# B step of a two-block recurrent transformer: Q b in one pass, half a's scores directly behind it, half b's maximum by a TensorE product, fewer mask and memory products, tail unit split

## The chip, the cores and the metric

The kernel runs on 1 core of one Trainium2 chip. The metric is the device time of one execution in microseconds (us). TensorE (PE) does the matrix products and writes PSUM; VectorE (DVE), ScalarE (ACT) and GpSimd (POOL) do the rest; SyncE (SP) issues most DMA.

## What is computed

Four layers A, B, A, B on x of [1, 2048, 640], each with a layer norm ahead and a residual sum behind. A is an attention in four segments with a linear memory; the change does not touch it. B is a segment recurrence, cut here to what matters:

```python
mem = mem0                                   # [1, 8, 640]
for s in range(n_seg):                       # 64 segments of 32 tokens
    h = concatenate([mem, xs], axis=1)       # 40 rows: 8 of memory, 32 of the segment
    q, k, v = h @ Wq, h @ Wk, h @ Wv         # 32 heads of 128
    scores = where(mask, q @ k.T * scale, -1e9)  # mask: row < 8 or row >= column
    p = softmax(scores)
    o = (p @ v) @ Wo
    mem = o[:, :M, :].copy()                 # the next step needs this
    outs.append(o[:, M:, :])
```

So the 64 steps of a B layer follow each other strictly: the memory rows of a step come out of its output product.

## The kernel before

A B step s (function layer_B, loop over 64 steps) holds the segment's columns as b_HX, [128, 5 chunks of 640, 32 columns]: 24 tokens known ahead and 8 memory columns written last. The other 8 tokens of each segment (the "tails") do not depend on the recurrence; they are projected ahead, four steps at once, by one "unit" a step: tail_unit (K or Q of a half, 20 products of 512 columns, PSUM tile b_tail, copied by ScalarE to b_tu in tail_evac and transposed by VectorE into b_tK or b_tQ in tail_turn) and vtail_unit (V, tile b_vtail, cut into pieces by vtail_some and stored by DMA). The output rows of the tails are deferred too (od_chunk, tile b_OPSd).

The 32 heads stand in two halves, a (0 to 15) and b (16 to 31). In PSUM, 32 rows of four column groups j carry four heads at a time: a product with tile_position=(0, 32 * j) uses the 128 x 32 part j of TensorE's array, and four of them run side by side (written 128*32 in the profile).

The order of a step on TensorE, ScalarE, VectorE and GpSimd is the order of the program: layer_B runs under _OrdNC, which chains the instructions of each engine. TensorE's order in a step before the change:

1. K a, Q a, K b (by_head, 20 products of 512 columns each: b_Ka, b_Qa, b_Kb), Q b in two passes of 256 columns (b_Qb in the ps pool, b_Qc in the tail buffer). kq copies each by ScalarE to b_kq, turn transposes it by VectorE into b_KT or b_QT.
2. mask_mm of half a (four 128*32 products of the identity with the mask, tile b_SP), one chunk of V a (thin_mm, b_Va), the 32 score products of half a (b_KT with b_QT and b_QZ), two chunks of V a, mask_mm and scores of half b with one chunk of V a between, the last chunk.
3. V b (b_Vb), od_chunk (b_OPSd), the whole tail unit (b_tail), and in some steps ln_spread (five 128*128 transposes, b_lntps).
4. pv of half a (b_OTP from b_PTa), pv of half b (from b_PTb): products of 32*128 and 8*128. Two chunks of vtail.
5. The output product (b_OPS, 64 products), the second part of od_chunk, then the memory rows: ScalarE copies three pieces of b_OPS to b_msb, TensorE sums and transposes each with the selection matrix selm (b_MT), VectorE copies it into the next step's b_HX; vtail chunks stand between.

The softmax of a half on the way from b_SP to b_PT: soft_max (VectorE, negated row maximum, b_negmax), soft_sub (VectorE, adds it into PSUM), soft_exp (ScalarE, b_E), soft_sum and soft_rec (VectorE, b_ssum, b_rs), soft_p (GpSimd, b_Pn), p_turn (two transposes on VectorE, b_PTa or b_PTb). VectorE's order before is: soft_max, soft_sub of a, then of b, then soft_sum and soft_rec of a and of b, then p_turn of a and b.

Layer-norm units: ln_begin (VectorE statistics) stands in steps with s % 4 == 1 (up to 57) and in three steps with s % 16 == 10, 18 of 64; ln_spread follows one step later. In steps 0 to 59 there is a tail unit to be kept, in 60 to 62 one runs without use, in 63 none.

Of the kernel before, what the change touches and what calls it, by code (L numbers as in the profile page):

```python
# [18 lines left out]
F32 = mybir.dt.float32  # L19
BF16 = mybir.dt.bfloat16  # L20
ACT = mybir.ActivationFunctionType
ALU = mybir.AluOpType
# [784 lines left out]
def layer_B(nc, tc, C, W, x_src, xb_src, x_dst, mem0, B_Wv, B_Wo, nsteps=64, out_bf16=False, tag=""):  # L807
# [6 lines left out]
    with ExitStack() as ctx:  # L814
# [26 lines left out]
        def ps_tile(shape, dtype, name):  # L841
            return pp.tile(shape, dtype, name=name, tag="ps")
# [72 lines left out]
        def thin_mm(cols_ap, Wt, b, name, c0=0, c1=NCH, ps=None):  # L915
            if ps is None:
                ps = ps_tile([128, 512], F32, name)
            for c in range(c0, c1):
                for j in range(4):
                    n = 4 * b + j  # L920
                    nc.tensor.matmul(ps[32 * j:32 * j + 32, :], lhsT=cols_ap[:, c, :], rhs=Wt[:, c, 512 * n:512 * n + 512],
                                     start=(c == 0), stop=(c == NCH - 1), tile_position=(0, 32 * j), skip_group_check=True)
            return ps

        def by_head(cols_ap, Wt, h0, nh, ps):
            for c in range(NCH):
                wt = Wt[:, c, 128 * h0:128 * (h0 + nh)].rearrange("p (h e) -> p h e", e=128)
                for j in range(4):
                    nc.tensor.matmul(ps[32 * j:32 * j + 32, :].rearrange("p (h x) -> p h x", x=32), lhsT=cols_ap[:, c, :], rhs=wt[:, :, 32 * j:32 * j + 32],
                                     start=(c == 0), stop=(c == NCH - 1), tile_position=(0, 32 * j), skip_group_check=True)  # L930
            return ps
# [16 lines left out]
        def tail_cols(g, c=None):  # L948
            v = TX[g // 4][:, :, 4 * (g % 4):4 * (g % 4) + 4, :].rearrange("p c s t -> p c (s t)")
            return v if c is None else v[:, c]  # L950

        def tail_unit(g, k, ps):
            proj, b = divmod(k, 2)
            return by_head(tail_cols(g), W.wq if proj else W.wk, 16 * b, 16, ps)

        def tail_evac(k, ps):
            sb = kqp.tile([128, 512], BF16, name="b_tu", tag="kq")
            evac("act", sb[:], ps[:], SCB if k // 2 else None)
            return sb
# [130 lines left out]
        for s in range(nsteps):  # L1090
# [11 lines left out]
            def kq(ps, scale=None, n=512, name="b_kq"):  # L1102
                sb = kqp.tile([128, n], BF16, name=name, tag="kq")
                evac("act", sb[:], ps[:], scale)
                return sb

            def turn(sb, D_, h0, nh):
                nc.vector.transpose(out=D_[s][:, h0:h0 + nh, 0:32], in_=sb[:].rearrange("p (h x) -> p h x", x=32))

            def mask_mm(b):  # L1110
                SP = ps_tile([128, 5, 40], F32, f"b_SP{b}")
                for j in range(4):
                    nc.tensor.matmul(SP[32 * j:32 * j + 32].rearrange("p g k -> p (g k)"), lhsT=C.identb[:, 32 * j:32 * j + 32], rhs=mask5[:].rearrange("p g k -> p (g k)"),
                                     start=True, stop=False, tile_position=(0, 32 * j), skip_group_check=True)
                return SP

            def scores(b, SP):
# [6 lines left out]
                            nc.tensor.matmul(SP[32 * j:32 * j + 32, 0 if tail else 1 + i, :], lhsT=lhsT, rhs=KT[s][:, h, :],  # L1124
                                             start=False, stop=True, tile_position=(0, 32 * j), skip_group_check=True)

            negmax = sm.tile([128, 2, 5], F32, name="b_negmax", tag="negmax")
            ssum = sm.tile([128, 2, 5], F32, name="b_ssum", tag="ssum")
            rs = sm.tile([128, 2, 5], F32, name="b_rs", tag="rs")
            E_ = wk.tile([128, 2, 5, 40], BF16, name="b_E", tag="E0")  # L1130

            def soft_max(b, SP):
                nc.vector.tensor_reduce(out=negmax[:, b, :], in_=SP[:], axis=AX.X, op=ALU.max, negate=True)

            def soft_sub(b, SP):
                nc.vector.tensor_tensor(out=SP[:], in0=SP[:], in1=negmax[:, b, :].unsqueeze(2).to_broadcast([128, 5, 40]), op=ALU.add)

            def soft_exp(b, SP):
                nc.scalar.activation(out=E_[:, b], in_=SP[:], func=ACT.Exp)

            def soft_sum(b):
                nc.vector.tensor_reduce(out=ssum[:, b, :], in_=E_[:, b], axis=AX.X, op=ALU.add)

            def soft_rec(b):
                nc.vector.reciprocal(out=rs[:, b, :], in_=ssum[:, b, :])

            def soft_p(eng, b):
                eng.tensor_tensor(out=Pn[:, b, :, 0:40], in0=E_[:, b], in1=rs[:, b, :].unsqueeze(2).to_broadcast([128, 5, 40]), op=ALU.mult)

            def p_turn(b, PT):  # L1150
                nc.vector.transpose(out=PT[:, :, :, 8:40], in_=Pn[:, b, 1:5, :].rearrange("p g (a k) -> p a g k", a=2))
                nc.vector.transpose(out=PT[:, :, :, 0:8], in_=Pn[:, b, 0, :].rearrange("p (a i t) -> p a i t", a=2, i=4))
# [19 lines left out]
            VH[s] = wkl.tile([128, 2, 512], BF16, name="b_Vth", tag="Vth")  # L1172
            for b in range(2):
                for nm, Wt, D_, scale in (("K", W.wk, KT, None), ("Q", W.wq, QT, SCB)):
                    if b and nm == "Q":
                        for e, q in enumerate((ps_tile([128, 256], F32, "b_Qb"), po.tile([128, 256], F32, name="b_Qc", tag="tail"))):
                            by_head(cols, Wt, 16 + 8 * e, 8, q)
                            turn(kq(q, scale, 256), D_, 16 + 8 * e, 8)
                    else:
                        ps = by_head(cols, Wt, 16 * b, 16, ps_tile([128, 512], F32, f"b_{nm}{'ab'[b]}"))  # L1180
                        turn(kq(ps, scale), D_, 16 * b, 16)
            SPa = mask_mm(0)
            Va = thin_mm(cols, W.wv, 0, "b_Va", 0, 1)
            scores(0, SPa)
            thin_mm(cols, W.wv, 0, "b_Va", 1, 3, Va)
            SPb = mask_mm(1)
            thin_mm(cols, W.wv, 0, "b_Va", 3, 4, Va)
            scores(1, SPb)
            thin_mm(cols, W.wv, 0, "b_Va", 4, NCH, Va)
            PTa = wkl.tile([128, 2, 4, 40], BF16, name="b_PTa", tag="PTa")  # L1190
            PTb = wkl.tile([128, 2, 4, 40], BF16, name="b_PTb", tag="PTb")
            soft_max(0, SPa)
            soft_sub(0, SPa)
            soft_exp(0, SPa)
            soft_max(1, SPb)
            soft_sub(1, SPb)
            soft_sum(0)
            soft_rec(0)
            soft_p(nc.gpsimd, 0)
            soft_exp(1, SPb)  # L1200
            evac("act", VH[s][:, 0, :], Va[:])
            soft_sum(1)
            soft_rec(1)
            soft_p(nc.gpsimd, 1)
            p_turn(0, PTa)
            p_turn(1, PTb)
            Vb = thin_mm(cols, W.wv, 1, "b_Vb")
            evac("act", VH[s][:, 1, :], Vb[:])
            if not last:
                od_chunk(0)  # L1210

            if work:
                tps = tail_unit(work[0], work[1], po.tile([128, 512], F32, name="b_tail", tag="tail"))
            if unit:
                tsb = tail_evac(unit[1], tps)
            if ln_ready:
                ln_spread(ln_ready.pop(0), po.tile([128, NCH, 4, 32], BF16, name="b_lntps", tag="ops"))
            if last:
# [9 lines left out]
            OTv = OTsb[:].rearrange("p (a x) -> p a x", a=2)  # L1228
            pv(0, PTa, ots)
            evac("dve", OTv[:, 0, 0:160], otf[0][:].rearrange("p i c -> p (i c)"))  # L1230
            ot01 = ps_tile([128, 4, 40], F32, "b_OTP1")
            ots[0][1] = ot01[:]
            pv(1, PTb, ots)
            evac("act", OTv[:, :, 160:320], otf[1][:].rearrange("p a i c -> p a (i c)"))
            evac("dve", OTv[:, 1, 0:160], ot01[:].rearrange("p i c -> p (i c)"))
            evac("act", OTv[:, :, 480:640], otf[3][:].rearrange("p a i c -> p a (i c)"))
            evac("dve", OTv[:, :, 320:480], otf[2][:].rearrange("p a i c -> p a (i c)"))
            if not last and (s + 1) % 4:
                vtails_in(s + 1)
# [17 lines left out]
            if not last:  # L1257
                dst = cols_of(s + 1)
                msb = wk.tile([128, 320], BF16, name="b_msb", tag="msb")
                parts = ((0, 1), (1, 3), (3, NCH))  # L1260
                for ca, cb in parts:
                    nc.scalar.copy(msb[:, 64 * ca:64 * cb], ops[:, 64 * ca:64 * cb])
                for pi, (ca, cb) in enumerate(parts):
                    mt = ps_tile([128, cb - ca, 8], F32, f"b_MT{pi}")
                    for c in range(ca, cb):
                        for q in range(4):
                            o = 64 * c + 32 * (q % 2)
                            nc.tensor.matmul(mt[32 * q:32 * q + 32, c - ca, :], lhsT=msb[:, o:o + 32], rhs=selm[:, q // 2, :],
                                             start=True, stop=True, tile_position=(0, 32 * q), skip_group_check=True)
                    nc.vector.tensor_copy(dst[:, ca:cb, 24:32], mt[:])  # L1270
                    vtail_some((1, 1, NCH)[pi])
            vtail_some(NCH)
# [114 lines left out]
```

## Time and profile before

| | |
|---|---|
| three timed runs, us | 2427.61, 2425.11, 2420.36 (median 2425.11) |
| the profiled execution, us | 2418.85 |
| its span, first to last instruction, us | 2417.1 |
| granted TensorE clock, mean | 0.997 |
| PE busy | 2289.2 us (95%), 62330 products |
| DVE busy | 1882.4 us (78%) |
| ACT busy | 1416.2 us (59%) |
| POOL busy | 749.8 us (31%) |
| the chain that ended last | PE 67%, DVE 14%, ACT 9%, DMA 4% of the span |

All of it comes from one profiled execution. A busy PE is not PE at its peak: products are pipelined, the profile's length of one product holds the time in which it drains (some 0.17 us), and the next of the same shape starts before that ends. In rows of the timeline the first two columns are the start in the span and the length of the merged row; x20 is the count of instructions in it; a bracket tells how long the engine had stood idle and what released it.

### The profile page before, as it was taken

The numbers are of one execution on the slowest core, as the hardware profiler recorded it, in microseconds if no ns is written. First come the engines' busy times: TensorE is split into PE (matmuls) and PEld (weight loads), VectorE is DVE, ScalarE is ACT, GpSimd is POOL, SyncE is SP. The second block draws the span as 40 slices with busy tenths as digits, with TensorE's granted clock in tenths as the row PEclk, the third lists the DMA queues.
The fourth block names the chain that finished last, engine by engine and source line by source line (L and its number), as shares of the span: only waits on it lengthen the run. The fifth ranks groups of instructions, "written<-read, shape, count | busy, mean of one in ns | idle before, by whom it ended". The sixth has DMA issues, their size and how long they took to land.

```text
span 2417.1 us, 139330 instructions
## 1 busy us (share of the span) xinstructions
PE 2289.2 (95%) x62330; PEld 1504.1 (62%) x62330; DVE 1882.4 (78%) x4695; ACT 1416.2 (59%) x3198; POOL 749.8 (31%) x1589
## 2 busy tenths in 40 slices
PE   8999999999999999999989999999999999999998
PEld 5566656666666666666655665566666666666665
DVE  8999877777777777777679998777777777777776
ACT  6999964444444444444369999644444444445443
POOL 5677641111111111111146776411111111111111
PEclk9999999999999999999999999999999999999999
DMA  4121271111111111111220211711111111111110
GB/s 168 47 85 60 73 260 27 28 32 32 29 30 30 31 29 32 29 31 28 65 88 17 64 45 38 274 24 26 29 28 27 27 27 28 27 29 29 27 24 20
DMA packets 168883, 123.38 MB, mean 51 GB/s; under 512 B 104652, under 2 KB 153180, under 8 KB 166492
## 3 DMA queue, kind: packets, MB, share of 16 engines
q1 hardware_dynamic: 167288, 112.69, 16.4%
q8 instruction: 487, 7.98, 1.4%
q10 hardware_dynamic: 996, 1.79, 0.2%
q14 instruction: 112, 0.92, 0.1%
HBM read 79.60 MB, written 34.80 MB: 47 GB/s over the span
## 4 chain that ended last, share of the span: by engine, by line
PE 67%; DVE 14%; ACT 9%; DMA 4%; issue 3%; POOL 1%; SPq 1%; ACTq 0%; DVEq 0%; POOLq 0%
PE b_OPS L113 11%; PE b_Ka L113 6%; PE b_Kb L113 5%; PE b_Qa L113 5%; DVE a_nm L142 5%; PE b_tail L113 5%; PE b_Va L113 4%; PE b_Vb L113 4%; ACT a_PT L142 4%; PE b_vtail L113 4%; PE a_S L113 3%; PE b_SP L113 2%; PE b_OPSd L113 2%; PE b_OTP L113 2%; PE b_Qb L113 2%
## 5 line engine op out<-in xcount | busy, mean ns | idle before, releaser
L113 PEld LDWEIGHTS <-b_HX 128*32 128x32 bf16 x17920 | 467.0, 96 | 269.0 <-DVE b_HX L113 3.6
L113 POOL TENSOR_TENSOR b_Pn<-b_E,b_rs 128x200 bf16<-128x200 bf16 x256 | 133.4, 522 | 1092.7 <-DVE b_rs L113 1074.6
L142 DVE TENSOR_REDUCE a_nm<-a_S 128x2 f32<-128x512 f32 (+3 forms) x512 | 395.4, 817 | 52.8 <-PE a_S L113 37.5
L142 ACT ACTIVATE a_PT<-a_T 128x1024 bf16<-128x1024 f32 (+1 forms) x384 | 345.5, 905 | 22.8 <-PE a_T L113 15.0
L113 PE MATMUL b_OPS<-b_wo,b_OTsb 128*32 128x320 bf16 x8192 | 306.5, 300 | 4.6 <-DVE b_OTsb L113 3.6
L113 PEld LDWEIGHTS <-b_OTsb 128*32 128x32 bf16 x8192 | 208.1, 96 | 73.8 <-DVE b_OTsb L113 24.8
L113 DVE STREAM_TRANSPOSE b_KT<-b_kq 128x512 bf16<-128x512 bf16 x256 | 181.3, 708 | 80.3 <-ACT b_kq L113 79.7
L142 POOL TENSOR_SCALAR_AFFINE_SELECT a_PT<-a_PT 128x256 bf16<-128x256 bf16 x380 | 189.3, 503 | 152.5 <-ACT a_PT L142 151.0
L113 ACT ACTIVATE b_E<-b_SP 128x200 bf16<-128x200 f32 x256 | 86.3, 337 | 235.5 <-DVE b_SP L113 225.4
L113 PE MATMUL b_Va<-b_wv,b_HX 128*32 128x512 bf16 x2560 | 222.4, 381 | 0.0
L113 DVE CAST b_HX<-b_MT 128x16 bf16<-128x16 f32 (+1 forms) x380 | 64.7, 172 | 198.3 <-PE b_MT L113 190.0
L113 DVE STREAM_TRANSPOSE b_QT<-b_kq 128x256 bf16<-128x256 bf16 (+1 forms) x384 | 184.2, 505 | 39.3 <-ACT b_kq L113 35.9
L113 ACT CAST b_msb<-b_OPS 128x64 bf16<-128x64 f32 x378 | 69.3, 256 | 213.2 <-PE b_OPS L113 213.2
L113 PEld LDWEIGHTS <-b_TX 128*32 128x32 bf16 x5360 | 144.1, 96 | 58.4 <-issue 5.3
L113 DVE CAST b_OTsb<-b_OTP 128x160 bf16<-128x160 f32 (+1 forms) x384 | 133.8, 376 | 44.7 <-PE b_OTP L113 40.8
L113 PE MATMUL b_Ka<-b_wk,b_HX 128*32 128x512 bf16 x2560 | 163.5, 381 | 1.0 <-DVE b_HX L113 0.9
L113 PE MATMUL b_Vb<-b_wv,b_HX 128*32 128x512 bf16 x2560 | 162.2, 379 | 0.0
L113 PE MATMUL b_Qa<-b_wq,b_HX 128*32 128x512 bf16 x2560 | 161.1, 379 | 0.0
L113 PE MATMUL b_Kb<-b_wk,b_HX 128*32 128x512 bf16 x2560 | 161.1, 379 | 0.0
L113 PE MATMUL b_vtail<-b_wv,b_TX 128*32 128x256 bf16 x2680 | 149.7, 273 | 1.3 <-issue 0.7
L113 ACT CAST b_kq<-b_Ka 128x512 bf16<-128x512 f32 x128 | 74.9, 585 | 123.0 <-PE b_Ka L113 123.0
L113 ACT CAST b_OTsb<-b_OTP 128x320 bf16<-128x320 f32 x256 | 96.5, 429 | 81.4 <-PE b_OTP L113 81.0
(185 smaller groups left out, 5048.3 us busy)
## 6 DMA issues: line engine op xcount, KB each, us to landing
b_wv<-in_B_Wv_dram SPq DMA_DIRECT2D x10, 1024.0 KB
b_wo<-in_B_Wo_dram SPq DMA_DIRECT2D x16, 640.0 KB
b_VT<-b_VTd SPq DMA_DIRECT2D x504, 16.0 KB
b_XO<-xres SPq DMA_DIRECT2D x256, 30.0 KB
b_VTd<-b_vt SPq DMA_DIRECT2D x480, 16.0 KB
b_xt<-xres_bf SPq DMA_DIRECT2D x40, 160.0 KB
b_wk<-in_B_Wk_dram SPq DMA_DIRECT2D x20, 256.0 KB
b_wq<-in_B_Wq_dram SPq DMA_DIRECT2D x20, 256.0 KB
```

The source lines that it names most:

```text
L113: r = f(*a, **k)
L142: r = f(*a, **k)
```

## The change

Q b is one pass of 512 columns in one PSUM tile, like the other projections. Its transpose on VectorE comes behind half a's mask, scores and maximum; V a follows in one piece, then mask and scores of half b. Half b's maximum is kept in bf16, and soft_sub of half b is a TensorE product of the identity with the broadcast maximum, accumulated onto b_SP between V b's third and fourth chunk. mask_mm is one 128 x 128 product in place of four of 128 x 32. The tail unit's chunks 0 to 2 stand ahead of pv of half a and chunks 3 and 4 between pv of half a and of half b; its ScalarE copy moves behind the value products' evacuations on ScalarE. p_turn of half a is issued ahead of soft_p of half b. b_MT is made of two 128 x 64 products a chunk in place of four of 128 x 32.

```diff
@@ -922,8 +922,8 @@
                                      start=(c == 0), stop=(c == NCH - 1), tile_position=(0, 32 * j), skip_group_check=True)
             return ps
 
-        def by_head(cols_ap, Wt, h0, nh, ps):
-            for c in range(NCH):
+        def by_head(cols_ap, Wt, h0, nh, ps, c0=0, c1=NCH):
+            for c in range(c0, c1):
                 wt = Wt[:, c, 128 * h0:128 * (h0 + nh)].rearrange("p (h e) -> p h e", e=128)
                 for j in range(4):
                     nc.tensor.matmul(ps[32 * j:32 * j + 32, :].rearrange("p (h x) -> p h x", x=32), lhsT=cols_ap[:, c, :], rhs=wt[:, :, 32 * j:32 * j + 32],
@@ -949,9 +949,9 @@
             v = TX[g // 4][:, :, 4 * (g % 4):4 * (g % 4) + 4, :].rearrange("p c s t -> p c (s t)")
             return v if c is None else v[:, c]
 
-        def tail_unit(g, k, ps):
+        def tail_unit(g, k, ps, c0=0, c1=NCH):
             proj, b = divmod(k, 2)
-            return by_head(tail_cols(g), W.wq if proj else W.wk, 16 * b, 16, ps)
+            return by_head(tail_cols(g), W.wq if proj else W.wk, 16 * b, 16, ps, c0, c1)
 
         def tail_evac(k, ps):
             sb = kqp.tile([128, 512], BF16, name="b_tu", tag="kq")
@@ -1109,9 +1109,8 @@
 
             def mask_mm(b):
                 SP = ps_tile([128, 5, 40], F32, f"b_SP{b}")
-                for j in range(4):
-                    nc.tensor.matmul(SP[32 * j:32 * j + 32].rearrange("p g k -> p (g k)"), lhsT=C.identb[:, 32 * j:32 * j + 32], rhs=mask5[:].rearrange("p g k -> p (g k)"),
-                                     start=True, stop=False, tile_position=(0, 32 * j), skip_group_check=True)
+                nc.tensor.matmul(SP[:].rearrange("p g k -> p (g k)"), lhsT=C.identb[:], rhs=mask5[:].rearrange("p g k -> p (g k)"),
+                                 start=True, stop=False, skip_group_check=True)
                 return SP
 
             def scores(b, SP):
@@ -1124,16 +1123,20 @@
                             nc.tensor.matmul(SP[32 * j:32 * j + 32, 0 if tail else 1 + i, :], lhsT=lhsT, rhs=KT[s][:, h, :],
                                              start=False, stop=True, tile_position=(0, 32 * j), skip_group_check=True)
 
-            negmax = sm.tile([128, 2, 5], F32, name="b_negmax", tag="negmax")
+            negmax = [sm.tile([128, 5], dt_, name=f"b_negmax{b}", tag=f"negmax{b}") for b, dt_ in enumerate((F32, BF16))]
             ssum = sm.tile([128, 2, 5], F32, name="b_ssum", tag="ssum")
             rs = sm.tile([128, 2, 5], F32, name="b_rs", tag="rs")
             E_ = wk.tile([128, 2, 5, 40], BF16, name="b_E", tag="E0")
 
             def soft_max(b, SP):
-                nc.vector.tensor_reduce(out=negmax[:, b, :], in_=SP[:], axis=AX.X, op=ALU.max, negate=True)
+                nc.vector.tensor_reduce(out=negmax[b][:], in_=SP[:], axis=AX.X, op=ALU.max, negate=True)
 
             def soft_sub(b, SP):
-                nc.vector.tensor_tensor(out=SP[:], in0=SP[:], in1=negmax[:, b, :].unsqueeze(2).to_broadcast([128, 5, 40]), op=ALU.add)
+                shift = negmax[b][:].unsqueeze(2).to_broadcast([128, 5, 40])
+                if b:
+                    nc.tensor.matmul(SP[:], lhsT=C.identb[:], rhs=shift, start=False, stop=True, skip_group_check=True)
+                else:
+                    nc.vector.tensor_tensor(out=SP[:], in0=SP[:], in1=shift, op=ALU.add)
 
             def soft_exp(b, SP):
                 nc.scalar.activation(out=E_[:, b], in_=SP[:], func=ACT.Exp)
@@ -1172,47 +1175,41 @@
             VH[s] = wkl.tile([128, 2, 512], BF16, name="b_Vth", tag="Vth")
             for b in range(2):
                 for nm, Wt, D_, scale in (("K", W.wk, KT, None), ("Q", W.wq, QT, SCB)):
-                    if b and nm == "Q":
-                        for e, q in enumerate((ps_tile([128, 256], F32, "b_Qb"), po.tile([128, 256], F32, name="b_Qc", tag="tail"))):
-                            by_head(cols, Wt, 16 + 8 * e, 8, q)
-                            turn(kq(q, scale, 256), D_, 16 + 8 * e, 8)
-                    else:
-                        ps = by_head(cols, Wt, 16 * b, 16, ps_tile([128, 512], F32, f"b_{nm}{'ab'[b]}"))
-                        turn(kq(ps, scale), D_, 16 * b, 16)
+                    ps = by_head(cols, Wt, 16 * b, 16, ps_tile([128, 512], F32, f"b_{nm}{'ab'[b]}"))
+                    sb = kq(ps, scale)
+                    if not (b and nm == "Q"):
+                        turn(sb, D_, 16 * b, 16)
             SPa = mask_mm(0)
-            Va = thin_mm(cols, W.wv, 0, "b_Va", 0, 1)
             scores(0, SPa)
-            thin_mm(cols, W.wv, 0, "b_Va", 1, 3, Va)
+            soft_max(0, SPa)
+            turn(sb, QT, 16, 16)
+            Va = thin_mm(cols, W.wv, 0, "b_Va")
             SPb = mask_mm(1)
-            thin_mm(cols, W.wv, 0, "b_Va", 3, 4, Va)
             scores(1, SPb)
-            thin_mm(cols, W.wv, 0, "b_Va", 4, NCH, Va)
+            soft_sub(0, SPa)
+            soft_max(1, SPb)
+            soft_exp(0, SPa)
+            Vb = thin_mm(cols, W.wv, 1, "b_Vb", 0, 3)
             PTa = wkl.tile([128, 2, 4, 40], BF16, name="b_PTa", tag="PTa")
             PTb = wkl.tile([128, 2, 4, 40], BF16, name="b_PTb", tag="PTb")
-            soft_max(0, SPa)
-            soft_sub(0, SPa)
-            soft_exp(0, SPa)
-            soft_max(1, SPb)
             soft_sub(1, SPb)
+            soft_exp(1, SPb)
+            thin_mm(cols, W.wv, 1, "b_Vb", 3, NCH, Vb)
             soft_sum(0)
             soft_rec(0)
             soft_p(nc.gpsimd, 0)
-            soft_exp(1, SPb)
             evac("act", VH[s][:, 0, :], Va[:])
             soft_sum(1)
             soft_rec(1)
+            p_turn(0, PTa)
             soft_p(nc.gpsimd, 1)
-            p_turn(0, PTa)
             p_turn(1, PTb)
-            Vb = thin_mm(cols, W.wv, 1, "b_Vb")
             evac("act", VH[s][:, 1, :], Vb[:])
             if not last:
                 od_chunk(0)
 
             if work:
-                tps = tail_unit(work[0], work[1], po.tile([128, 512], F32, name="b_tail", tag="tail"))
-            if unit:
-                tsb = tail_evac(unit[1], tps)
+                tps = tail_unit(work[0], work[1], po.tile([128, 512], F32, name="b_tail", tag="tail"), 0, 3)
             if ln_ready:
                 ln_spread(ln_ready.pop(0), po.tile([128, NCH, 4, 32], BF16, name="b_lntps", tag="ops"))
             if last:
@@ -1228,12 +1225,16 @@
             OTv = OTsb[:].rearrange("p (a x) -> p a x", a=2)
             pv(0, PTa, ots)
             evac("dve", OTv[:, 0, 0:160], otf[0][:].rearrange("p i c -> p (i c)"))
+            if work:
+                tail_unit(work[0], work[1], tps, 3, NCH)
             ot01 = ps_tile([128, 4, 40], F32, "b_OTP1")
             ots[0][1] = ot01[:]
             pv(1, PTb, ots)
             evac("act", OTv[:, :, 160:320], otf[1][:].rearrange("p a i c -> p a (i c)"))
             evac("dve", OTv[:, 1, 0:160], ot01[:].rearrange("p i c -> p (i c)"))
             evac("act", OTv[:, :, 480:640], otf[3][:].rearrange("p a i c -> p a (i c)"))
+            if unit:
+                tsb = tail_evac(unit[1], tps)
             evac("dve", OTv[:, :, 320:480], otf[2][:].rearrange("p a i c -> p a (i c)"))
             if not last and (s + 1) % 4:
                 vtails_in(s + 1)
@@ -1263,10 +1264,9 @@
                 for pi, (ca, cb) in enumerate(parts):
                     mt = ps_tile([128, cb - ca, 8], F32, f"b_MT{pi}")
                     for c in range(ca, cb):
-                        for q in range(4):
-                            o = 64 * c + 32 * (q % 2)
-                            nc.tensor.matmul(mt[32 * q:32 * q + 32, c - ca, :], lhsT=msb[:, o:o + 32], rhs=selm[:, q // 2, :],
-                                             start=True, stop=True, tile_position=(0, 32 * q), skip_group_check=True)
+                        for q in range(2):
+                            nc.tensor.matmul(mt[64 * q:64 * q + 64, c - ca, :], lhsT=msb[:, 64 * c:64 * c + 64], rhs=selm[:, q, :],
+                                             start=True, stop=True, tile_position=(0, 64 * q), skip_group_check=True)
                     nc.vector.tensor_copy(dst[:, ca:cb, 24:32], mt[:])
                     vtail_some((1, 1, NCH)[pi])
             vtail_some(NCH)
```

## The prediction

> **What bounds the kernel now.** I read the page first, then the chain of waits in the middle of the second B layer, then the timeline of each engine over one step. The span:
>
> ```profile
> span 2417.1 us, 139330 instructions
> ```
>
> The profiled execution took 2418.85 us, 1.75 us more than this span. The three timed runs have a median of 2425.11 us, 0.3% above it; 0.3%, some 7 us, is also the least difference that a measurement here can tell from none. My sums start from 2418.85.
>
> Two layers of 64 B steps fill most of the span. One step on TensorE's timeline, from its K product to the next one's, with the end of the step in full (columns: start in us, length in us):
>
> ```profile
> 1825.93 1.26 PE L113 MATMUL b_Ka<-b_wk,b_HX 128*32 128x512 bf16 x20
> ...
> 1838.16 0.45 PE L113 MATMUL b_OPSd<-b_wo,b_OTdef 128*32 128x320 bf16 x8
> 1838.44 0.28 PE L113 MATMUL b_vtail<-b_wv,b_TX 128*32 128x256 bf16 x4
> 1838.65 0.19 PE L113 MATMUL b_MT<-b_sel,b_msb 128*32 128x8 bf16 x4
> 1838.69 0.28 PE L113 MATMUL b_vtail<-b_wv,b_TX 128*32 128x256 bf16 x4
> 1838.82 0.21 PE L113 MATMUL b_MT<-b_sel,b_msb 128*32 128x8 bf16 x8
> 1838.89 0.28 PE L113 MATMUL b_vtail<-b_wv,b_TX 128*32 128x256 bf16 x4
> 1839.00 0.21 PE L113 MATMUL b_MT<-b_sel,b_msb 128*32 128x8 bf16 x8
> 1839.12 1.26 PE L113 MATMUL b_Ka<-b_wk,b_HX 128*32 128x512 bf16 x18
> ```
>
> A step takes 1839.12 - 1825.93 = 13.19 us. The chain of waits through the same step:
>
> ```profile
> 1829.35 0.55 PE b_Qb L113 x19
> 1829.90 0.54 PE b_Qc L113 x19
> 1830.44 0.09 PE b_SP L113 x4
> ...
> 1833.53 1.09 PE b_tail L113 x20
> ...
> 1835.42 0.38 PE b_OTP L113 x32
> ```
>
> TensorE has no gap until the tail unit ends at 1834.62. The second value product (the b_OTP at 1835.42) then waits for the softmax, which is VectorE's chain:
>
> ```profile
> 1830.08 0.71 DVE L113 STREAM_TRANSPOSE b_KT<-b_kq 128x512 bf16<-128x512 bf16 x1 [0.35 <-ACT b_kq L113]
> 1830.71 0.73 DVE L113 STREAM_TRANSPOSE b_QT<-b_kq 128x256 bf16<-128x256 bf16 x2
> 1831.47 0.37 DVE L113 TENSOR_REDUCE b_negmax<-b_SP 128x5 f32<-128x200 f32 x1
> 1831.88 0.37 DVE L113 TENSOR_TENSOR b_SP<-b_SP,b_negmax 128x200 f32<-128x200 f32 x1
> ...
> 1833.39 0.36 DVE L113 TENSOR_REDUCE b_ssum<-b_E 128x5 f32<-128x200 bf16 x1
> 1833.78 0.19 DVE L113 RECIPROCAL b_rs<-b_ssum 128x5 f32<-128x5 f32 x1
> 1834.12 0.57 DVE L113 STREAM_TRANSPOSE b_PTa<-b_Pn 128x256 bf16<-128x256 bf16 x2
> 1834.70 0.57 DVE L113 STREAM_TRANSPOSE b_PTb<-b_Pn 128x256 bf16<-128x256 bf16 x2
> ```
>
> VectorE works without a pause from 1830.08 to 1835.27, and b_OTP starts 0.15 us later. So two paths are nearly balanced: TensorE's full order, and VectorE's chain, which makes TensorE wait some half a microsecond.
>
> **The price that decides: a change of tile shape on TensorE.** Three places of the timeline, two of TensorE around a step with a layer-norm unit and one at the start of the first B layer. The figure before the sizes (128*32, 128*128, 32*128) is the part of the array that a product occupies:
>
> ```profile
> 1807.61 0.62 PE L113 MATMUL b_tail<-b_wq,b_TX 128*32 128x512 bf16 x8
> 1808.16 0.45 PE L113 MATMUL b_lntps<-c_identb,b_xt 128*128 128x128 bf16 x5
> 1808.55 0.20 PE L113 MATMUL b_OTP<-b_PTa,b_Vth 32*128 32x40 bf16 x4
> ...
> 1809.22 0.20 PE L113 MATMUL b_OTP<-b_PTb,b_VT 8*128 8x40 bf16 x4
> 1809.39 0.40 PE L113 MATMUL b_vtail<-b_wv,b_TX 128*32 128x256 bf16 x8
> ```
>
> ```profile
> 341.78 0.84 PE L113 MATMUL a_YP<-a_wo,a_oTx 128*128 128x320 bf16 x5 [0.37 <-DVE a_late L142]
> 342.55 2.34 PE L113 MATMUL b_tail<-b_wk,b_TX 128*32 128x512 bf16 x39
> ```
>
> Between products of one shape, the next starts 0.17 us before the last has ended: OPSd ends at 1838.16 + 0.45 = 1838.61 and vtail starts at 1838.44. Where the shape changes the overlap shrinks: b_tail (128*32) ends at 1808.23 and b_lntps (128*128) starts at 1808.16, 0.07 before; from b_lntps to b_OTP 0.06; from b_OTP back to 128*32 0.03 (1809.42 against 1809.39); from the A layer's 128*128 to b_tail's 128*32 0.07 (342.62 against 342.55). A change of shape thus costs TensorE 0.10, 0.11, 0.14 and 0.10 us. I take 0.11.
>
> The Trainium skill has this as a rule ("TensorEngine Tiling (Array Packing)", Tiling Modes, Key Properties): changing the tiling mode, and not just the tile, drains TensorE. The trace agrees for the three shapes above; the page also lists 128×64 as a mode of its own, which no row here shows.
>
> **The change part by part**, for a step without a layer-norm unit, in the times of the step at 1825.93.
>
> Q b in one pass: 1.08 like the other 512-wide products (Vb to OPSd or Ka to the next), in place of 0.55 + 0.54. -0.01 us; Q b ends at 1830.43.
>
> Masks: four 128*32 products side by side (0.09) become one 128*128 product. It streams the same 200 columns, so again 0.09, but the array changes to the full shape and back: +0.22 each, twice, +0.44. None of it is hidden: TensorE has work queued on both sides.
>
> Half a's scores directly behind Q b: 1830.43 + 0.31 (mask) + 0.23 for 32 score products, as now, gives 1830.97. VectorE's maximum of half a then comes before the transpose of Q b. That transpose waits for ScalarE's copy, 0.60 us long from about 1830.53:
>
> ```profile
> 1828.39 0.60 ACT L113 ACTIVATE b_kq<-b_Qa 128x512 bf16<-128x512 f32 x1 [0.50 <-PE b_Qa L113]
> ...
> 1833.02 0.34 ACT L113 ACTIVATE b_E<-b_SP 128x200 bf16<-128x200 f32 x1 [0.32 <-DVE b_SP L113]
> ```
>
> So: maximum at 1831.04, transpose of Q b from 1831.4 to 1832.1. Queued behind it on VectorE are half a's subtraction and half b's maximum. TensorE meanwhile does all of Va (1.08, to 1832.05) and the second mask (to 1832.36), so half b's scores do not wait; they end at 1832.59.
>
> Half b's maximum by a TensorE product: VectorE loses one subtraction (0.38), TensorE gains a full-shape product of 200 columns: 0.09 + 0.22 = +0.31. It is placed behind 12 of Vb's 20 products (0.65). The maximum of half b is ready at about 1833.03, before TensorE arrives at 1833.24, so nothing waits for it, and what is queued behind it (the rest of Vb) is not held up. The product ends at 1833.44. The shift is a broadcast operand of step 0, of which no row shows the speed: at worst I allow a second 0.09, at best nothing more.
>
> From there the chain to the second value product: exponential of half b about 0.10 later, 1833.54; its sum 0.37 after that start (1833.02 to 1833.39 now), 1833.91; reciprocal 0.39 on, 1834.30; transposes of half a behind it from 1834.49 to 1835.06 (GpSimd's product of half a is finished by then); those of half b 0.92 after the reciprocal's start, as now, 1835.22 to 1835.79.
>
> TensorE: the tail unit's first 12 products end at 1834.62 - 0.01 + 0.44 + 0.31 - 0.43 = 1834.93. The first value product waits for its transposes: 1835.06 + 0.05 = 1835.11, and ends at 1835.49. Then the shape changes to 128*32 for the tail unit's last 8 products (0.11 + 0.43, to 1836.03) and back (0.11, less the overlap of 0.17): the second value product starts at 1835.97, now bound by TensorE and not by VectorE (1835.79 + 0.15 = 1835.94). Against 1835.42 that is +0.55 us. What stood in TensorE's wait before is more than used up.
>
> The memory products (b_MT) become half as many, each 128*64, between vtail products of 128*32. The first change of shape is free: b_vtail's four products take 0.11 (1838.89 to 1839.00), so TensorE is idle by 1838.55 and b_MT waits until 1838.65 for ScalarE. Five changes remain before the next Ka: 0.55. Against it stand 0.08 for halved products (half of 0.04 + 0.07 + 0.05) and 0.07 of slack before Ka, which waits for the first b_HX copy. +0.40 us. Bounds: -0.02 if 64 columns need no change, +0.55 at 0.14 a change. I take 0.11, the row nearest to it, since every change of columns in the trace costs about that.
>
> The tail unit's ScalarE copy and VectorE transpose (0.70) move behind the evacuations of the value products, some 0.73 us later in VectorE's queue. Queued behind are a layer-norm unit's statistics, where there is one, and the b_HX copies that release the next step. VectorE there now:
>
> ```profile
> 1798.70 0.15 DVE L113 TENSOR_SCALAR b_ln_rstd<-b_ln_mv 128x1 f32<-128x1 f32 x1
> 1799.34 0.59 DVE L113 CAST b_HX<-b_MT 128x8 bf16<-128x8 f32 x3 [0.48 <-PE b_MT L113]
> ```
>
> The 0.48 of idle time is overrun by 0.24 us. While TensorE loses 0.40 in the same place this is covered; without that it costs 0.24 in 36 steps, 9 us. No queue of DMA is moved.
>
> In a step with a layer-norm unit spread (18 of a layer's 64) the five b_lntps products (0.45 - 0.17 = 0.28, and 0.11 for the shape) stand ahead of the first value product: first tail part 1834.93, b_lntps 1835.32, value product from 1835.26 to 1835.64, tail 1836.18, second value product 1836.12, +0.70.
>
> Sum: 45 steps of 0.55 + 0.40 = 0.95 and 18 of 1.10 in each layer, 42.8 + 19.8 = 62.6, in two layers 125 us. 2418.85 + 125 = 2544; I take off some 4 us for waits on DMA that a longer step lets pass, an estimate: **2540 us**.
>
> **Rivals.**
>
> *The 64-column shape needs no drain.* Only rows of 128, 32 and 8 by 128 and of 128 by 32 stand in the trace, so nothing there excludes it. Then 126 x 0.40 = 50 us go, and the covered 9 us of the layer-norm steps come out: 2540 - 50 + 9 = 2499 us. Chance 0.20.
>
> *Each change costs what b_OTP to b_vtail shows, 0.14.* There are 13 on the path (two for each mask, two for half b's shift, two for the split tail unit, five at b_MT): 13 x 0.03 x 126 = 49 us more, 2590 us. For it: small products stand on one side of most of these changes, as there. Chance 0.10.
>
> *The changes are free in these places, and it is faster.* Half b's shift then ends at 1830.43 + 0.09 + 0.23 + 1.08 + 0.09 + 0.23 + 0.65 + 0.09 = 1832.89, the second value product starts 2.50 us later as above, 1835.39: 0.03 gained, because VectorE's chain is only re-ordered, and 0.08 at b_MT. 0.11 x 126 = 14 us, less 9 for the layer-norm steps; with a VectorE chain tighter by 0.1 us a step, 2400 us. It decides only where a change costs under 0.11 / 13 = 0.01 us, and four rows say ten times that. Chance 0.07, of which 0.02 lies within 0.3%.
>
> *Fewer instructions are the gain.* A step loses 20 + 6 + 10 products and gains 1, 35 net. If each instruction cost what the b_OTP products take at most, 0.38 / 32 = 0.012 us, that were 0.42 us a step, 53 us, and 2366 us. But the chain shows 0.55 + 0.54 for 40 products against 1.09 for 20 of b_tail: the columns count, not the instructions. Chance 0.01. The Trainium skill, "TensorE: Matmul & The Clock Gate" (Back-to-back issue gap), gives a floor of about 25 ns from start to start; by it the 35 products were 0.9 us a step, and the rows above disagree.
>
> **How the numbers follow.** Forecast 0.62, rivals 0.20, 0.10, 0.07 and 0.01. The range takes in the first rival (2499, with some tolerance for the unknown shift and lags) and most of the second: 2485 to 2590. Faster by over 0.3%: 0.06; within: 0.02; slower: 0.92.
>
> **What would show it.** Right: steps of about 14.1 us; b_SP's single mask products starting only 0.07 us before the last product's end, and the same at b_MT; TensorE without a wait ahead of the second value product, its start 10.0 us after Ka's; some 57,900 TensorE products. Wrong: steps of 13.2 us or less; a b_MT of 128*64 that overlaps its neighbours by 0.17 us (first rival); a wait for b_negmax at the shift product.

## The result, and the profile after

The changed kernel takes 2539.02 us (median of four runs, 2536.66 to 2542.85) against 2426.36 for the kernel before (four runs): 1.0474 times as long, 95% interval 1.0448 to 1.0500. The forecast was 2540 in a range of 2485 to 2590.

The page after: the span, the first line of the engines, the chain that ended last.

```profile
span 2538.7 us, 129782 instructions
...
PE 2441.0 (96%) x57870; PEld 1392.1 (55%) x57870; DVE 1822.8 (72%) x4439; ACT 1399.0 (55%) x3070; POOL 751.8 (30%) x1589
...
PE 77%; DVE 10%; ACT 7%; DMA 3%; issue 2%; SPq 0%; POOL 0%; ACTq 0%; DVEq 0%; POOLq 0%
```

TensorE runs 4460 products fewer and is busy 152 us longer; its share of the chain rises from 67% to 77%. One step on TensorE's timeline (start, length, operation; the shape stands before the sizes):

```profile
1943.10 1.26 PE L113 MATMUL b_Ka<-b_wk,b_HX 128*32 128x512 bf16 x20
...
1946.35 1.25 PE L113 MATMUL b_Qb<-b_wq,b_HX 128*32 128x512 bf16 x20
1947.53 0.26 PE L113 MATMUL b_SP<-b_mask,c_identb 128*128 128x200 bf16 x1
1947.72 0.28 PE L113 MATMUL b_SP<-b_KT,b_QT 128*32 128x40 bf16 x16
...
1949.56 0.84 PE L113 MATMUL b_Vb<-b_wv,b_HX 128*32 128x512 bf16 x12
1950.33 0.26 PE L113 MATMUL b_SP<-b_negmax,c_identb 128*128 128x200 bf16 x1
1950.52 0.62 PE L113 MATMUL b_Vb<-b_wv,b_HX 128*32 128x512 bf16 x8
...
1951.23 0.82 PE L113 MATMUL b_tail<-b_wq,b_TX 128*32 128x512 bf16 x12
1952.17 0.20 PE L113 MATMUL b_OTP<-b_PTa,b_Vth 32*128 32x40 bf16 x4
...
1952.48 0.61 PE L113 MATMUL b_tail<-b_wq,b_TX 128*32 128x512 bf16 x8
1953.03 0.20 PE L113 MATMUL b_OTP<-b_PTb,b_Vth 32*128 32x40 bf16 x4
...
1956.05 0.28 PE L113 MATMUL b_vtail<-b_wv,b_TX 128*32 128x256 bf16 x4
1956.27 0.20 PE L113 MATMUL b_MT<-b_sel,b_msb 128*64 128x8 bf16 x2
1956.40 0.29 PE L113 MATMUL b_vtail<-b_wv,b_TX 128*32 128x256 bf16 x4
1956.62 0.23 PE L113 MATMUL b_MT<-b_sel,b_msb 128*64 128x8 bf16 x4
1956.78 0.29 PE L113 MATMUL b_vtail<-b_wv,b_TX 128*32 128x256 bf16 x4
1957.00 0.23 PE L113 MATMUL b_MT<-b_sel,b_msb 128*64 128x8 bf16 x4
1957.16 0.40 PE L113 MATMUL b_Ka<-b_wk,b_HX 128*32 128x512 bf16 x4
```

The step takes 1957.16 - 1943.10 = 14.06 us instead of 13.19. Wherever the shape changes the overlap has shrunk: Q b ends at 1947.60 and the mask starts 0.07 before; b_vtail ends at 1956.33 and b_MT starts 0.06 before (there it waits for ScalarE anyway), later at 1956.69 against 1956.62, 0.07. Two b_vtail pieces with a b_MT between them started 0.20 us apart before (1838.69, 1838.89) and start 0.38 apart now (1956.40, 1956.78). From the second value product to the next K a there are 4.13 us (1953.03 to 1957.16) instead of 3.70.

VectorE in the same step:

```profile
1949.82 0.37 DVE L113 TENSOR_REDUCE b_negmax<-b_SP 128x5 bf16<-128x200 f32 x1 [0.28 <-PE b_SP L113]
...
1951.39 0.19 DVE L113 RECIPROCAL b_rs<-b_ssum 128x5 f32<-128x5 f32 x1
1951.50 0.53 DVE L113 STREAM_TRANSPOSE b_PTa<-b_Pn 128x256 bf16<-128x256 bf16 x2
1952.31 0.57 DVE L113 STREAM_TRANSPOSE b_PTb<-b_Pn 128x256 bf16<-128x256 bf16 x2 [0.28 <-POOL b_Pn L113]
```

The maximum is ready at 1950.19, before TensorE comes to its product at 1950.33. VectorE now has idle time in brackets where it had none; TensorE reaches the second value product just as half b's transposes are done (1952.88).

### The profile page after: what moved, and what is told of

It reads as the page before. It is cut to its first block, busy times and chain, and to the rows that moved or that the text cites. A ratio compares the mean times of both kernels' runs of the same rounds, so it can differ in the third digit from the quotient of the medians.

```text
span 2538.7 us, 129782 instructions
## 1 busy us (share of the span) xinstructions
PE 2441.0 (96%) x57870; PEld 1392.1 (55%) x57870; DVE 1822.8 (72%) x4439; ACT 1399.0 (55%) x3070; POOL 751.8 (30%) x1589
## 4 chain that ended last, share of the span: by engine, by line
PE 77%; DVE 10%; ACT 7%; DMA 3%; issue 2%; SPq 0%; POOL 0%; ACTq 0%; DVEq 0%; POOLq 0%
PE b_OPS L113 11%; PE b_SP L113 6%; PE b_Ka L113 6%; PE b_Vb L113 5%; PE b_tail L113 5%; PE b_Va L113 5%; PE b_Qb L113 5%; PE b_Kb L113 5%; PE b_Qa L113 5%; DVE a_nm L142 5%; PE b_vtail L113 4%; ACT a_PT L142 4%; PE b_OTP L113 3%; PE a_S L113 2%; PE b_OPSd L113 2%; PE b_MT L113 2%
## 5 line engine op out<-in xcount | busy, mean ns | idle before, releaser
L113 PEld LDWEIGHTS <-b_HX 128*32 128x32 bf16 x15360 | 390.3, 96 | 305.8 <-issue 2.1
L113 PE MATMUL b_OPS<-b_wo,b_OTsb 128*32 128x320 bf16 x8192 | 311.6, 301 | 12.8 <-issue 8.9
L113 PEld LDWEIGHTS <-c_identb 128*128 128x128 bf16 x1312 | 107.6, 98 | 204.7 <-issue 180.5
L113 DVE STREAM_TRANSPOSE b_QT<-b_kq 128x512 bf16<-128x512 bf16 x256 | 180.7, 706 | 43.5 <-ACT b_kq L113 43.5
L113 PE MATMUL b_Vb<-b_wv,b_HX 128*32 128x512 bf16 x2560 | 186.8, 382 | 0.0
L113 PE MATMUL b_vtail<-b_wv,b_TX 128*32 128x256 bf16 x2680 | 166.2, 278 | 0.0
L113 PE MATMUL b_Va<-b_wv,b_HX 128*32 128x512 bf16 x2560 | 163.2, 380 | 0.6 <-ACT b_kq L113 0.6
L113 PE MATMUL b_Qb<-b_wq,b_HX 128*32 128x512 bf16 x2560 | 160.5, 379 | 0.0
```

The lines of the kernel that those rows point to most:

```text
L113: r = f(*a, **k)
```

## The experiments

A time stands beside that of the kernel before in the same set of runs. The changed kernel's 2539.02 is of another set (2426.36 there, 2422.21 beside the kernels with a part undone), so a difference under some 4 us from it means nothing. A step is counted from K a to K a; "median step" is that of the ordinary steps, without layer-norm work. What a kernel does in a step is read from its one profiled execution.

**The price of a change of shape by itself.** Before Q a and K b of the kernel before stands one more product of 8 columns, once in each of three shapes:

```diff
+ if (b, nm) in ((0, "Q"), (1, "K")):
+     nc.tensor.matmul(ps[0:w, 0:8], lhsT=C.identb[:, 0:w], rhs=mask5[:, 0, 0:8], ...)   # w = 32, 64, 128
  by_head(cols, Wt, 16 * b, 16, ps)
```

> The kernel before with one more product of 8 columns, of shape 128*32, ahead of Q a and of K b in each step (its result is overwritten). No change of shape. Theory: at most some 0.02 us for each, 0 to 5 us more than 2426. Rival (any added instruction with its weights costs 0.1 us): 126 x 0.2 = 25 us more.

> The same with the two products of shape 128*64. Theory (64 columns are a shape of their own): four changes of 0.10 to 0.12 us a step, 50 to 60 us over the kernel before, 2476 to 2486. Rival (64 columns need no change): as with 128*32, 2426 to 2431.

> The same with the two products of shape 128*128. Theory: four changes of 0.10 to 0.12 us a step, 50 to 60 us over the kernel before, 2476 to 2486, the same as 128*64. Rival (the cost is in loading more columns of weights): about twice that of 128*64.

Measured: 2428.96, 2480.26 and 2477.62 us against 2423.70. K a, the added product and Q a with 32, 64 and 128 columns:

```profile
1848.45 1.26 PE L113 MATMUL b_Ka<-b_wk,b_HX 128*32 128x512 bf16 x20
1849.54 0.17 PE L113 MATMUL b_Qa<-b_mask,c_identb 128*32 128x8 bf16 x1
1849.54 1.26 PE L113 MATMUL b_Qa<-b_wq,b_HX 128*32 128x512 bf16 x20
```

```profile
1881.86 1.26 PE L113 MATMUL b_Ka<-b_wk,b_HX 128*32 128x512 bf16 x20
1883.05 0.19 PE L113 MATMUL b_Qa<-b_mask,c_identb 128*64 128x8 bf16 x1
1883.18 1.26 PE L113 MATMUL b_Qa<-b_wq,b_HX 128*32 128x512 bf16 x20
```

```profile
1881.34 1.26 PE L113 MATMUL b_Ka<-b_wk,b_HX 128*32 128x512 bf16 x20
1882.53 0.18 PE L113 MATMUL b_Qa<-b_mask,c_identb 128*128 128x8 bf16 x1
1882.64 1.26 PE L113 MATMUL b_Qa<-b_wq,b_HX 128*32 128x512 bf16 x20
```

From K a to Q a there are 1.09, 1.32 and 1.30 us. 64 and 128 columns cost the same, 51 and 49 us more than 32 columns: over 128 steps of four changes 0.10 us a change. The rival that 64 columns need no change falls, and so does the one by which the weights' size counts.

**Each part undone in the changed kernel.** First the memory rows:

```diff
-for q in range(2):  # 64 columns each
+for q in range(4):  # 32 columns each, as before
```

> The changed kernel with the memory rows made by four 128*32 products a chunk again. Theory: from the second value product to the next K a there are 4.13 us now and 3.70 before; all of it is changes between 64 and 32 columns, so 0.40 to 0.43 us a step return, 50 to 54 us, less about 0.2 us in 36 layer-norm steps (7 us), where VectorE's later queue takes the place: 2489 to 2496. Rival (the later tail copy and transpose on ScalarE and VectorE delay the next step): little returns, 2530 to 2539. Rival (64 columns need no change of shape): also about 2539.

Measured 2496.76 us (the kernel before 2422.21 in this set): 42 us returned, just short of the expectation (2489 to 2496). The stretch from b_MT to the next K a goes, in the median, from 0.89 back to 0.47 us, in steps with layer-norm statistics to 0.62: VectorE's later queue is there, with 0.15 us.

```diff
-nc.tensor.matmul(SP[:]..., lhsT=C.identb[:], rhs=mask5[:]..., start=True, stop=False, ...)
+for j in range(4): nc.tensor.matmul(SP[32*j:32*j+32]..., lhsT=C.identb[:, 32*j:32*j+32], ..., tile_position=(0, 32*j), ...)
```

> The changed kernel with its two mask products made of four 128*32 products each again. Theory (a change of shape costs TensorE about 0.1 us; the change's two mask products cost 0.18 to 0.20 us each): TensorE gets back 0.36 to 0.40 us a step, but half b's scores can come at most 0.18 earlier before they wait for VectorE's transpose of Q b (it ends at 1949.28 and the scores start at 1949.34 in the changed kernel). So 0.18 to 0.36 us a step, 23 to 45 us less than 2539: 2494 to 2516. Rival (the softmax order, not the shapes, costs the time): nothing, 2539.

Measured 2526.31: only 13 us returned, less than expected. So neither the theory's range nor the rival (nothing) holds. The shortest steps did shrink by 0.29 us (14.06 to 13.77), inside the expectation, but the mean step only by 0.10. Most of what came in between is below (standstills).

```diff
-negmax in (F32, BF16); half b: nc.tensor.matmul(SP[:], lhsT=C.identb[:], rhs=shift, start=False, stop=True, ...)
+negmax in (F32, F32); half b: nc.vector.tensor_tensor(out=SP[:], in0=SP[:], in1=shift, op=ALU.add)
```

> The changed kernel with half b's maximum (f32) subtracted by VectorE again, in the same order. TensorE loses a product that cost it 0.30 us. Theory (this stretch is now held by the softmax chain too: the first value product starts right after its transposes): on VectorE the subtraction adds about 0.4 us ahead of half a's sum, so half a's transposes come 0.1 to 0.3 us later, and the first value product, tail part and second value product with them: 2550 to 2575. Rival (TensorE's sum of products alone sets the step): 0.30 us a step less, 38 us, 2501.

Measured 2573.60, in the range expected: slower by 35 us, though TensorE has a product less. The timeline of VectorE there:

```profile
1947.82 0.37 DVE L113 TENSOR_REDUCE b_negmax<-b_SP 128x5 f32<-128x200 f32 x1 [0.46 <-PE b_SP L113]
1948.22 0.38 DVE L113 TENSOR_TENSOR b_SP<-b_SP,b_negmax 128x200 f32<-128x200 f32 x1
1948.50 0.35 DVE L113 TENSOR_REDUCE b_ssum<-b_E 128x5 f32<-128x200 bf16 x1
...
1949.45 0.19 DVE L113 RECIPROCAL b_rs<-b_ssum 128x5 f32<-128x5 f32 x1
1949.78 0.57 DVE L113 STREAM_TRANSPOSE b_PTa<-b_Pn 128x256 bf16<-128x256 bf16 x2
```

Half a's transposes start 1.96 us after half b's maximum instead of 1.68 (1949.82 to 1951.50), because half a's sum now queues behind the subtraction; the first value product, the tail piece behind it and the second value product follow. In this order the TensorE product is worth its price.

```diff
-tps = tail_unit(..., 0, 3)   ...   tail_unit(work[0], work[1], tps, 3, NCH)
+tps = tail_unit(...)
```

> The changed kernel with the tail unit in one piece ahead of the first value product; its copy and transpose stay where the change put them. TensorE has two changes of shape less (0.22 us). Theory: the second value product starts at 1953.03, and half b's transposes end at 1952.88, 0.15 before; so the softmax chain holds it at the same time in ordinary steps and nothing is won there; in the 36 steps with a layer-norm spread the order of TensorE binds by 0.2 us, up to 7 us: 2531 to 2539. Rival (each change of shape counts in full wherever it stands): 0.22 us x 126 = 28 us less, 2511.

Measured 2532.35, 7 us less, in the range expected. Beside the kernel before in the same set it is 1.0452 times as long (1.0432 to 1.0473), which is not clear of the changed kernel's 1.0474 (1.0448 to 1.0500). Two changes of shape less, but ordinary steps still take 14.06: TensorE waits instead.

**The order alone.** All shapes back to 32 columns, the new order kept:

```diff
 (memory rows and masks as in the two experiments above)
-nc.tensor.matmul(SP[:], lhsT=C.identb[:], rhs=shift, ...)
+for j in range(4): nc.tensor.matmul(SP[32*j:32*j+32], lhsT=C.identb[:, 32*j:32*j+32], rhs=shift, ..., tile_position=(0, 32*j), ...)
```

> The changed kernel with its order kept and every product that it made wider put back to shape 128*32: masks, memory rows, and half b's maximum as four 128*32 products on TensorE. Theory: the shapes carry the whole loss; what is left is the order, worked out at 0.03 us a step better than before, and the layer-norm steps 0.2 us worse, so 2420 to 2436, no more than 0.4% from the kernel before. Rival (the order, the split tail unit or the moved copy costs time): 2450 or more.

Measured 2475.72 against 2423.70, 1.021 (1.0192 to 1.0229). The theory that the shapes carry the whole loss falls: what stays of the change without its shapes (the order, with the split tail unit and the moved copy) costs 52 us, and the rival holds. Three pieces make up most of it. First, the shortest step is 13.28 instead of 13.16, 0.1 us or some 14 us in all: half b's scores now wait for the transpose of Q b. Weight loads of TensorE (PEld): one that waits, and all such waits in that kernel (us in total, times, longest):

```profile
1909.97 0.17 PEld L113 LDWEIGHTS <-b_QT 128*32 128x32 bf16 x16 [0.32 <-DVE b_QT L113]
```

```profile
PEld L113 <- DVE b_QT L113: 53.9, 136, 1.7
```

The same wait sums up to 4.0 us in the kernel before and in the changed one, where the slower masks covered it. Second, the layer-norm steps, 0.15 us in 36 of them, 5 us. Third, standstills inside b_OPS; the chain of waits:

```profile
1914.38 1.40 PE b_OPS L113 x40
1915.78 1.45 issue
1917.22 1.00 PE b_OPS L113 x24
```

"issue" is time in which TensorE waited for nothing that the profile shows. The stretch from b_OPS to b_OPSd takes 2.21 or 2.22 us in the median in every kernel. Its mean over all steps that have it is 2.21 in the kernel before, 2.29 in the changed one, 2.36 with the masks undone, 2.44 here: 0.23 us a step over the kernel before, some 27 us. The standstills come in a rhythm: about every 7th step here (400 TensorE products in an ordinary step), every 14th with the memory rows undone (391), every 23rd with the masks undone (387); with the changed kernel's 381 they bunch, most of them at the end of the second B layer. (The kernel before has 416; the counts 388, 407, 420 and 427 in expectations below are 4 to 7 too high.)

**Where the standstills come from.**

```diff
 (all_32_whole: all shapes put back, and the tail unit whole as above)
 (before_split: in the kernel before, tail_unit in two pieces around pv of half a, its copy behind the evacuations)
```

> The changed kernel with all shapes put back to 128*32 and the tail unit whole. Theory (the split brings the standstills inside b_OPS): their 0.26 us a step go, 30 us: 2440 to 2450, with steps of 13.3 us. Rival (the standstills hang on the count of TensorE's instructions in a step, which moves every seventh step into the same place): they stay, some 2470.

> The kernel before with only the tail unit split around the first value product and its copy moved behind the evacuations. Theory: the first value product starts at its old time, behind it 8 tail products and two more changes of shape put the second 0.86 us later instead of 0.68, +0.18 us a step, 23 us; besides, b_OPS stretches with a standstill that the profile lays to no engine are expected, as in the changed kernel and in the one with all shapes put back (0.07 to 0.26 us a step in the mean), 9 to 30 us: 2455 to 2477. Rival (the standstills come from the count of instructions in a step, not from the split): 2440 to 2450.

Measured 2466.29 and 2446.31 (the kernel before 2422.18). Both theories fall and their rivals hold: the split does not bring the standstills. They stay without it, every seventh step (mean 2.33), and in the kernel before with it the stretch is 2.26 in the mean. The split itself costs the 0.18 us a step that were worked out (13.37 against 13.19): in the old order, where the second value product waits anyway, 24 us.

```diff
+for e in range(n_):   # all_32_two: Q b in two passes of 256 columns, 20 products more
+    by_head(cols, Wt, 16 * b + 8 * e, 16 // n_, ps[:, 256 * e:512 if e or n_ == 1 else 256])
```

> The changed kernel with all shapes put back, the tail unit whole, and Q b in two passes of 256 columns again (into one PSUM tile, one copy and one transpose as before): 20 TensorE products more a step, 427, and 0.01 us of columns. All waits and the order stay. Theory (the standstills inside b_OPS hang on TensorE's count of instructions: with 388 + 6 + 3 + 10 = 407 products a step they come back about every seventh step): the count of the kernel before is nearly reached (420), the seven-step beat goes, and with it most of 0.2 us a step: 2440 to 2450. Rival (the re-ordered scores and softmax bring them): 2464 to 2472, standstills as before.

Measured 2476.00 (before 2421.93), above both ranges and nearer to the rival. The rhythm does change with the count, to three or four steps, but the time does not come back: b_OPS's mean stays 2.34.

What TensorE waits for in a standstill can be read from the traces. The pages list a DMA queue that carries instructions, in packets of 16 KB; its rows in the kernel before, the changed one and the one with all shapes put back (packets, MB, share):

```profile
q8 instruction: 487, 7.98, 1.4%
q8 instruction: 453, 7.42, 1.2%
q8 instruction: 472, 7.73, 1.3%
```

These kernels have 62330, 57870 and 60282 products and as many weight loads, 255 or 256 of TensorE's instructions for each packet. Counted along TensorE's order, the standstills inside b_OPS that no semaphore ends stand whole numbers of packets apart: 2809 products are 22 packets, 5490 with the memory rows undone are 43, and 8937 with the masks undone are 70, 127.7 products each time. Three packets hold 383 products, so in the changed kernel's steps of 381 to 386 the place where a packet begins hardly moves, and the more products a step has beyond that, the shorter the rhythm.

The landings fit too. In the chain above a packet's transfer started at 1914.62 and landed at 1915.78, and TensorE went on at 1917.22, 1.44 us later; over the 30 standstills of that kernel this takes 1.2 to 1.6 us, and in no B step of thirteen traces does the first product of a packet start less than 1.17 us after the landing. So TensorE stands still because its next instructions have come late. Summed over all places where a packet landed within 1.7 us of its use, TensorE's gap there exceeds the usual gap at the same place of a step by some 10 us in the kernel before and in the changed one, 21 with the memory rows undone, 28 with the masks undone and 36 with all shapes put back. So the two parts undone that returned less than expected lost 11 and 18 us to it. Why packets come later, against their use, in the new order than in the old is not shown and stays open.

**A part of the change in the old kernel.** Half b's shift by four 128*32 products:

```diff
 soft_max(1, SPb)
+Vb = thin_mm(cols, W.wv, 1, "b_Vb", 0, 3)
 soft_sub(1, SPb)            # now four 128*32 products of the identity with the bf16 maximum
+thin_mm(cols, W.wv, 1, "b_Vb", 3, NCH, Vb)
```

> The kernel before with one part of the change and no change of shape: half b's maximum (bf16) is subtracted by four 128*32 products between V b's third and fourth chunk. VectorE loses one subtraction (0.39 us to the next operation's start) from the chain that ends in the second value product; TensorE gains 0.09 us, which its wait of about 0.4 us ahead of that product hides. Theory (shapes cost, the idea itself is sound): half b's exponential starts 0.1 to 0.2 us earlier, the second value product 0.05 to 0.12 us, 6 to 15 us less in 126 steps: 2408 to 2418. Rival (a subtraction on TensorE costs more than on VectorE through the hand-over from engine to engine): 2424 or more.

Measured 2419.70 against 2422.18, 0.9989 (0.9976 to 1.0001): not to be told from no change, and between the two ranges. The median step fell to 13.12, 0.07 less as expected, but in steps with a layer-norm spread (13.27 against 13.25) TensorE's order binds, and there the added 0.09 us counts.

## Why the prediction was right

The level held, and so did the price of a change of shape. That the shapes carry the loss held only in part: with every wider product put back to 32 columns, the kernel is still 2.1% longer than the one before instead of 4.7%, and with the tail unit whole besides, 1.8%. The forecast had the new order at a gain of 0.03 us a step without its changes of shape. Against the steps of the forecast:

- Price of a change of shape, taken as 0.11 from four rows: the probes say 0.10, for 64 columns too. The first rival (64 columns free) falls, and with the measured time the second (0.14, 2590 us). The Trainium skill, "TensorEngine Tiling (Array Packing)", Tiling Modes, says that a change of mode drains TensorE and lists 128×64 as a mode of its own: the trace agrees, with 0.10 us for it.
- Masks +0.44: measured 0.40 (0.09 ahead of the first, 0.31 up to V b).
- Half b's shift +0.31: 0.33 (V b to the tail unit 1.68 us against 1.35). No wait for the maximum, as worked out.
- Second value product +0.55: +0.44 (9.93 us after K a against 9.49). This term was over-sized: beside the masks' 0.04, half a's transposes start 0.11 us behind the reciprocal's start and not 0.19, and the first value product comes 9.07 after K a, not 9.18.
- Memory rows +0.40: +0.43 in the step, 42 us when undone.
- Layer-norm spread steps +1.10: +1.01 (14.26 against 13.25). The forecast had counted from the ordinary step's 13.19.
- The step +0.95: +0.87. Two layers of 45 steps of 0.87 and 18 of 1.01 make 115 us and not 125; the spans differ by 121.6. Where the forecast took 4 us off for waits on DMA, some 7 us came on top instead, with longer standstills in b_OPS (0.08 us a step) among what changed. Two errors of 10 and 11 us against each other brought the level so near; that part is luck.

One rival was worked out wrongly, though it did not come about: with free changes of shape the new order was to be 0.03 us a step better. With the shapes put back it is 52 us worse. The failing step is half b's scores "do not wait": without the slow masks they wait for the transpose of Q b; and the standstills, some 27 us of the 52, were not in the sum at all.

So the loss is not a sum of parts. Undone one by one, they return 42 (memory rows), 13 (masks) and 7 us (split, not clear of noise) and -35 (shift): what one part takes, another hides, and standstills take a share.

## What to carry to other kernels

Fewer and wider products were no gain here, where the array is kept in narrow pieces: read in the timeline how far a product starts before the last one's end, and price each change of shape with what is missing there, going in and coming out. A product that stands in for a VectorE operation can pay where VectorE's chain ends last: in the changed kernel it was worth 35 us in spite of its two changes of shape; in the old order, in its neighbours' shape, its gain was not clear of noise. Check an order without its suspected cost before calling that cost the whole loss.

## What the runs showed of the hardware that was not expected

TensorE stands still inside a run of ready products for 0.3 to 1.8 us, in b_OPS always where a new 16 KB packet of its own instructions begins (about every 256 instructions) unless a semaphore ends the wait, and more in some orders than in others. In the kernel with all shapes put back the shortest step is 13.28 us and the mean step 13.81; in the kernel before they are 13.16 and 13.35 (steps with layer-norm work included). A lone 8-column product in its neighbours' shape cost 5.3 us in 256 places, 0.02 us each (ratio 1.0009 to 1.0039), while 20 more products of 256 columns a step in place of 512 cost 9.7 us in 128 steps, 0.004 us each, a figure that also holds whatever they changed in the standstills.
